# Gated linear attention with a mixture of adapters: loads of v on ScalarE's ring, a gate from negated logits, and a new instruction order

## The chip, the cores and the metric

The kernel runs on one core of one Trainium2 chip. The metric is the device time of one execution in microseconds. TensorE is called PE, VectorE DVE, ScalarE ACT, GpSimd POOL and SyncE SP, as in the profile.

## The reference

Four batches of eight heads, 768 steps, head size 48. First a linear attention with a decay `alpha` for each channel, then a mixture of eight rank-16 adapters, of which each token takes the two with the largest logits.

```python
for t in range(S):
    state = alpha[:, :, t, :, None] * state + np.einsum('bhd,bhe->bhde', k[:, :, t], v[:, :, t])
    y[:, :, t] = np.einsum('bhd,bhde->bhe', q[:, :, t], state)
x = y.transpose(0, 2, 1, 3).reshape(B * S, H * D)        # 3072 x 384
logits = x @ w_gate                                      # 3072 x 8
topk = the 2 largest of each row;  w = softmax over these 2
out = x + sum over the 2 of  w * ((x @ A[e]) @ B[e])
```

## The kernel before, in words

The sequence of a batch is cut into six chunks of 128 steps, so there are 24 units (batch, chunk), numbered `u`. Each unit passes through some thirty stages, each a small function of the same name in the code.

- `ld` loads a whole batch of one input (alpha as `a_t`, then `k_t`, `q_t`, `v_t`), 1.18 MB in runs of 48 floats. There are sixteen loads. `load_engine` says which engine issues each; before, that is SP for all of them. Each input has two buffers (`TURNS`), so a load of batch b waits for the readers of batch b - 2.
- `ln` takes the logarithm of two chunks of alpha (ACT). `cum` sums it along the chunk with a matmul (PE). `eup`, `edn` and `edec` are exponents of the sums (ACT). `kgm` and `qgm` multiply k and q with them, and `vbc` casts v (POOL).
- `tr` transposes kg and qg into one PSUM tile (PE, eight transposes). `kk` copies the k half out (DVE, L481), `qq` the q half (ACT, L486).
- `at` is the score product of a unit, eight matmuls on 48 rows each, two heads side by side in the upper and the lower rows of the array (L510). `msk` applies the causal mask (DVE, L518).
- `sdm` scales the state `kv` of the unit before into `sdec` (DVE, L462), and `kv` adds this unit's k times v (PE, L495 and L500).
- `yt` makes the output transposed: for a chunk after the first four full-size matmuls with `sdec` (L529), then eight matmuls on 64 columns each, two heads side by side in the columns of the array (L534). `xs` copies it to SBUF (ACT).
- `z` is the product with the adapters' A and with the gate (PE). The gate is a chain over the eight logits of a row: `gmx` (the eight values sorted, L571), `gdf` (minus the largest, L576), `gex` (exponent on ACT, L581), `gwu` (keep the two largest, and sum, L587), `grd` (reciprocal), `gzw` (weights times z).
- `zt` transposes that, `zs` copies it (ACT), `qs` and `av` make the untransposed output in the same PSUM bank (L548, L557), `delta` adds the product with B (L618), `fin` copies the sum (ACT, L625), and a store on SP sends it.

Matmuls thus come in three shapes of the array: full, row-tiled (`at`) and column-tiled (the second part of `yt`).

The order of every engine's instructions is written out ahead by a planner. `graph` builds a node for each stage and unit, with the costs in `STAGES` (engine, time on the engine, time to the result, in ns), dependencies from `CHAINS` and buffer reuse from `RINGS`. `list_order` takes the nodes one by one: of those that can begin within 40 ns of the first one it takes the one with the smallest key, unit number minus `LEAD` of the stage. Six PSUM slots are shared by `cum`, `tr`, `kv`, `yt`, `z` and `zt`; `HOLDS` names the readers that free them. Each engine runs its list in order. Semaphore waits are added where data or buffers need them, so the plan fixes the order, and not the times.

At the start four loads are issued from `early`, the adapters' weights come over POOL's queue (`wload`), and `wcast` casts them (DVE). SP's list is the sixteen loads, and then the 24 stores.

Of the kernel before, what the change touches and what calls it, by code (L numbers as in the profile page):

```python
# [30 lines left out]
NU = B * NCH  # L31

# [6 lines left out]
def _bc_mid(src: bass.AP, reps) -> bass.AP:  # L39
# [6 lines left out]
    "ln": ("ACT", 445, 545), "ln2": ("ACT", 765, 865),  # L46
    "cum": ("PE", 300, 466), "edn": ("ACT", 385, 485), "eup": ("ACT", 360, 485),
    "edec": ("ACT", 98, 172), "kgm": ("POOL", 979, 1024), "qgm": ("POOL", 979, 1024),
    "vbc": ("POOL", 461, 506), "tr": ("PE", 450, 620), "kk": ("DVE", 345, 429), "qq": ("ACT", 467, 592),
    "sdm": ("DVE", 497, 581), "kv": ("PE", 340, 500), "at": ("PE", 400, 570),  # L50
    "msk": ("DVE", 1164, 1248), "qs": ("PE", 170, 340), "av": ("PE", 215, 385),
    "yt": ("PE", 460, 630), "xs": ("ACT", 520, 612),
    "z": ("PE", 240, 410), "gmx": ("DVE", 91, 175),
    "gdf": ("DVE", 76, 160), "gex": ("ACT", 107, 232), "gwu": ("DVE", 268, 352),
    "grd": ("DVE", 71, 155), "gzw": ("DVE", 258, 342), "zt": ("PE", 57, 220),
    "zs": ("ACT", 147, 272), "delta": ("PE", 163, 330), "fin": ("ACT", 385, 485),
    "st": ("DMA", 655, 2455),
}
LEAD = {
    "kk": -24.77, "qq": -57.8, "vld": 4.5, "vbc": -57.63, "ln": -134.22, "cum": 14.46,  # L60
    "edn": -17.16, "eup": 17.71, "edec": -44.09, "kgm": 72.83, "qgm": -0.48, "tr": 63.33,
    "kq": -190.71, "sdm": -26.53, "kv": 46.61, "at": 13.93, "msk": -49.61, "qs": -13.02,
    "av": -10.13, "xb": 0.5, "xt": 0.4, "xs": -111.93, "z": 10.45, "zc": -33.57, "gmx": 8.16,
    "gdf": -28.3, "gex": 94.59, "gwu": -38.76, "grd": 76.82, "gw": -7.12, "gzw": -20.75,
    "yt": 41.02, "zt": 22.93, "zs": -73.06, "delta": 44.96, "fin": 36.34, "st": 100,
}
CHAINS = (
    "ln cum eup kgm tr kk at msk yt xs z gmx gdf gex gwu grd gzw zt zs delta fin st",
    "cum edn qgm tr", "cum edec sdm kv", "kgm kv", "vbc kv", "sdm yt", "tr qq at", "qq yt",
# [4 lines left out]
    ("tr", "qgm", QRING), ("kv", "vbc", VRING), ("av", "vbc", VRING), ("at", "kk", 3), ("at", "qq", 8), ("av", "qq", 8),  # L74
    ("msk", "at", 1), ("av", "msk", 5), ("z", "xs", 3), ("delta", "zs", 3), ("st", "fin", 24),
    ("qs", "sdm", SRING), ("kv", "sdm", 1), ("kgm", "cum", 4), ("qgm", "cum", 4), ("at", "tr", 8),
    ("av", "tr", 8), ("z", "yt", 3), ("delta", "zt", 3), ("st", "zt", 24),
# [4 lines left out]
    "yt": (("xs", 0),), "z": (("gzw", 0),), "zt": (("fin", 0),),  # L82
# [7 lines left out]
def list_order(nodes, deps, holds):  # L90
# [19 lines left out]
    order, span = [], 0  # L110
    for _ in nodes:
        best = None
        for e, names in cand.items():
            can = []
            for n in names:
                if n[0] == "ld" and loads[e][nl[e]][1] != n:
                    continue
                s = max(ready[n], free[e])
                if n in holds:
                    if slot[ns % SLOTS] is None:  # L120
                        continue
                    s = max(s, slot[ns % SLOTS])
                can.append((s, n))
# [15 lines left out]
        free[e] = s + nodes[n][1]  # L139
        end = s + nodes[n][2]  # L140
# [34 lines left out]
def load_engine(x):  # L175
    return "ACT" if x in ((0, 1, 0), (0, 3, 0)) else "SP"


def graph(lead):
    nodes, deps = {}, []  # L180

    def has(f, u):
        c = u % NCH
        if not 0 <= u < NU or (f in ("sdm", "edec", "qs") and c == 0):
            return False
# [28 lines left out]
    for x, item in enumerate(load_list()):  # L214
# [3 lines left out]
        t = 1060 if c is not None else 4450  # L218
        nodes[n] = ("DMB" if eng == "POOL" else "DMA", t, t + 1300, x)
# [3 lines left out]
        if eng == "POOL":  # L223
            nodes["is", x] = ("POOL", 1000, 1000, b * NCH + (c or 0) - 6)
            deps.append((("is", x), n))
            n = ("is", x)
        if b >= TURNS[i]:
# [6 lines left out]
    for f, readers in HOLDS.items():  # L234
        for u in range(NU):
            if (f, u) in nodes:
# [24 lines left out]
def kernel(  # L261
# [18 lines left out]
    trsb = ctx.enter_context(tc.tile_pool(name="trsb", bufs=8))  # L280
# [49 lines left out]
    def wcast(_):  # L330
        for hh in range(2):
# [4 lines left out]
            nc.vector.tensor_copy(  # L336
                W[rows, :, E * R:NW], W_st[rows, E * NP * R:].rearrange("f (p e) -> f p e", p=NP))
# [8 lines left out]
    early = [n for n in order if n[0] == "ld"][:4]  # L346
    for n in early:
        ld(n[1])
    nc.scalar.preload_act_table_set("natural_log_exp_and_others")
# [128 lines left out]
    def kk(u):  # L478
        s = st[u]
        s["kk"] = trsb.tile([P, NP, P], F2, name="kk", bufs=3)  # L480
        nc.vector.tensor_copy(out=s["kk"], in_=s["tr"][:, 0])  # L481

    def qq(u):
        s = st[u]
        s["qq"] = trsb.tile([P, NP, P], F2, name="qq")
        nc.scalar.copy(s["qq"], s["tr"][:, 1])  # L486
# [17 lines left out]
    def at(u):  # L504
        s = st[u]
        t = ps_at.tile([P, 2, NP, P], F4, name="at")
        for p in range(NP):
            for hh in range(2):
                rows = slice(HP * hh, HP * hh + D)
                nc.tensor.matmul(  # L510
                    t[:, hh, p, :], s["kk"][rows, p, :], s["qq"][rows, p, :],
# [10 lines left out]

    def yt(u):
        s = st[u]
        b, c = units[u]
        s["yt"] = ps_s.tile([P, NP, P], F4, name="yt", tag="m", bufs=6)
        if c > 0:
            for p in range(NP):
                nc.tensor.matmul(  # L529
                    s["yt"][:, p, :], sdec[u % SRING][:, p].rearrange("p b d -> p (b d)"),  # L530
                    s["qq"][:, p, :], start=(p == 0), stop=False, skip_group_check=True)
# [12 lines left out]
    def qs(u):  # L544
        s = st[u]
        b, c = units[u]
        for p in range(NP):
            nc.tensor.matmul(  # L548
                s["y"][:, p * 2 * D:(p + 1) * 2 * D], s["qq"][:, p, :],
# [23 lines left out]
    def gdf(u):  # L573
        s = st[u]
# [95 lines left out]
```

## Time and profile before

| | |
|---|---|
| median of 3 runs | 107.2 us (106.11 to 107.24) |
| profiled execution | 107.46 us, span 105.8 us |
| PE, matmul | 76.5 us busy, 72% of the span |
| ACT | 74.0 us, 70% |
| DVE | 70.0 us, 66% |
| POOL | 65.3 us, 62% |
| hardware DMA queue | 23.60 MB, 75.0% of 16 engines |
| granted PE clock | 0.998 |

The profile is of one execution. Its span runs from the first to the last instruction, and the device time lies 1.66 us above it. A row of the timeline has the start in us from the span's start, the length, the engine, the line of the code, the operation and its operands. A mark x8 means that eight instructions were merged. A bracket gives idle time of the engine before the row, and the event that ended it. DMA-issuing instructions are on a line of the queue's own (SPq for SP). Matmuls overlap, so the start of the next group tells more than the length of a row.

### The profile page before, as it was taken

To read this page: it belongs to the slowest core of one execution; us is meant where nothing else is said; L and a number is where in the kernel's file an instruction comes from. 1 tells how busy PE (TensorE), PEld (TensorE's weight loads), DVE (VectorE), ACT (ScalarE), POOL (GpSimd) and SP (SyncE) were. 2 spreads that over 40 slices of the span, in tenths; PEclk is the share of its full clock that TensorE was granted. 3 is DMA by queue.
4 is the path that set the end of the run, shared out by engine and by line. 5 is a ranking of instruction groups with operands and counts; after the bars stand their busy time and mean duration, and the time that the engine had idled before them with its cause. 6 is when DMAs were issued, how large, how long until landed. Compare 5 with 4: busy or idle time off the path is not lost.

```text
span 105.8 us, 3378 instructions
## 1 busy us (share of the span) xinstructions
PE 76.5 (72%) x1312; PEld 58.1 (55%) x1312; DVE 70.0 (66%) x229; ACT 74.0 (70%) x201; POOL 65.3 (62%) x103
## 2 busy tenths in 40 slices
PE   0007002397898898989999779889989999798850
PEld 0004001375575775757767568676767777676720
DVE  4002030159989797777998397979678999798810
ACT  4029900095889888896899789696995997665670
POOL 7992029989911959995191999940688794900000
PEclk9999999999999999999999999999999999999999
DMA  0999997979793989789896969698889899421052
GB/s 7 289 209 273 244 286 214 290 212 312 196 287 103 307 223 288 214 246 254 241 286 199 308 172 308 191 287 229 240 263 339 281 336 390 178 80 74 6 209 89
DMA packets 28528, 24.21 MB, mean 229 GB/s; under 512 B 752, under 2 KB 28400, under 8 KB 28512
## 3 DMA queue, kind: packets, MB, share of 16 engines
q1 hardware_dynamic: 28288, 23.60, 75.0%
q0 software_dynamic: 224, 0.41, 2.5%
q8 instruction: 10, 0.16, 0.6%
q14 instruction: 6, 0.05, 0.2%
HBM read 19.28 MB, written 4.72 MB: 227 GB/s over the span
## 4 chain that ended last, share of the span: by engine, by line
DMA 33%; PE 23%; SPq 10%; DVE 10%; ACT 10%; POOL 7%; issue 3%; ACTq 0%; POOLq 0%; DVEq 0%
DMA k_t<-in_k_dram 12%; DMA a_t<-in_alpha_dram 11%; SPq L306 10%; DMA q_t<-in_q_dram 10%; PE tr L475 5%; DVE at_sb L518 4%; POOL qg L450 4%; POOL kg L443 3%; PE yt L534 3%; PE z L565 2%; PE at L510 2%; ACT o L625 2%; ACT qq L486 2%; PE yt L529 2%; ACT zs L614 2%
## 5 line engine op out<-in xcount | busy, mean ns | idle before, releaser
L443 POOL TENSOR_TENSOR kg<-k_t,up 128x384 bf16<-128x384 f32 x24 | 23.7, 1004 | 17.2 <-DMA k_t<-in_k_dram 11.2
L518 DVE TENSOR_TENSOR at_sb<-at,mask 128x1024 bf16<-128x1024 f32 x24 | 29.2, 1217 | 0.7 <-PE at L510 0.6
L450 POOL TENSOR_TENSOR qg<-q_t,dn 128x384 bf16<-128x384 f32 x24 | 23.6, 1006 | 4.7 <-DMA q_t<-in_q_dram 2.4
L486 ACT COPY qq<-tr 128x512 bf16<-128x512 bf16 x24 | 14.2, 594 | 13.2 <-DVE kk L481 11.4
L481 DVE COPY kk<-tr 128x512 bf16<-128x512 bf16 x24 | 9.9, 421 | 12.1 <-PE tr L475 8.3
L542 ACT CAST xs<-yt 128x512 bf16<-128x512 f32 x24 | 14.4, 607 | 3.6 <-PE yt L534 3.6
L409 PE MATMUL cum<-lg,suf 128*128 128x384 bf16 x24 | 8.7, 369 | 8.2 <-ACT lg L400 8.2
L457 POOL CAST vb<-v_t 128x384 bf16<-128x384 f32 x24 | 11.7, 511 | 4.5 <-PE y L557 4.2
L475 PE MATMUL tr<-ident,kg 128*128 128x128 bf16 x96 | 9.9, 230 | 6.2 <-POOL kg L443 6.2
L400 ACT ACTIVATE lg<-a_t 128x768 bf16<-128x768 f32 x12 | 10.1, 860 | 6.1 <-DMA a_t<-in_alpha_dram 6.1
L475 PE MATMUL tr<-ident,qg 128*128 128x128 bf16 x96 | 9.8, 228 | 5.1 <-POOL qg L450 4.8
L625 ACT COPY o<-y 128x384 f32<-128x384 f32 x24 | 11.5, 496 | 1.3 <-PE y L618 1.0
L424 ACT ACTIVATE up<-cum 128x384 f32<-128x384 f32 x24 | 11.6, 504 | 0.3 <-PE cum L415 0.3
L429 ACT ACTIVATE dn<-cum 128x384 f32<-128x384 f32 x24 | 11.5, 508 | 0.0
L510 PE MATMUL at<-qq,kk 48*128 48x128 bf16 x192 | 9.8, 222 | 2.0 <-DVE at_sb L518 1.0
L462 DVE TENSOR_TENSOR sdec<-kv,dec 128x384 bf16<-128x384 f32 x20 | 10.9, 547 | 0.3 <-PE kv L500 0.3
L475 PEld LDWEIGHTS <-kg 128*128 128x128 bf16 x96 | 6.3, 101 | 7.4 <-POOL kg L443 6.3
L565 PE MATMUL z<-W,xs 128*128 128x136 bf16 x96 | 9.5, 223 | 1.0 <-ACT xs L542 0.6
L475 PEld LDWEIGHTS <-qg 128*128 128x128 bf16 x96 | 6.3, 102 | 6.8 <-POOL qg L450 6.8
L534 PE MATMUL yt<-at_sb,vb 128*64 128x128 bf16 x192 | 9.9, 225 | 0.0
L557 PE MATMUL y<-vb,at_sb 128*128 128x48 bf16 x192 | 8.7, 183 | 0.4 <-ACT zs L614 0.4
L618 PE MATMUL y<-B_all,zs 128*128 128x384 bf16 x24 | 7.7, 327 | 1.1 <-ACT zs L614 1.0
(58 smaller groups left out, 152.7 us busy)
## 6 DMA issues: line engine op xcount, KB each, us to landing
out_dram<-o SPq DMA_DIRECT2D x24, 192.0 KB, 2.3
W_st<-in_moe_A_dram POOLq DMA_DIRECT2D x2, 96.0 KB, 6.1
B_st<-in_moe_B_dram POOLq DMA_DIRECT2D x1, 192.0 KB, 6.9
a_t<-in_alpha_dram SPq DMA_DIRECT2D x4, 0.2 KB, 10.3
k_t<-in_k_dram SPq DMA_DIRECT2D x4, 0.2 KB, 10.9
q_t<-in_q_dram SPq DMA_DIRECT2D x4, 0.2 KB, 10.9
v_t<-in_v_dram SPq DMA_DIRECT2D x4, 0.2 KB, 10.5
W_st<-in_moe_w_gate_dram POOLq DMA_DIRECT2D x2, 6.0 KB, 5.5
```

The costliest lines, as they stand in the source:

```text
L424: nc.scalar.activation(s["up"].rearrange("p h d -> p (h d)"), s["cum"][:, 0:DM], AF.Exp)
L443: nc.gpsimd.tensor_tensor(out=s["kg"][:, :, 0:D], in0=batches[b][1][:, c], in1=s["up"], op=ALU.mult)
L450: nc.gpsimd.tensor_tensor(out=s["qg"][:, :, 0:D], in0=batches[b][2][:, c], in1=s["dn"], op=ALU.mult)
L457: nc.gpsimd.tensor_copy(out=s["vb"][:, :, 0:D], in_=batches[b][3][:, c])
L475: nc.tensor.transpose(t[:, w, p, :], pair(src, p), ident[:, :])
L486: nc.scalar.copy(s["qq"], s["tr"][:, 1])
L510: nc.tensor.matmul(t[:, hh, p, :], s["kk"][rows, p, :], s["qq"][rows, p, :], start=True, stop=True)
L518: nc.vector.tensor_tensor(out=s["at_sb"].rearrange("p a b t -> p (a b) t"), in0=s["at"].rearrange("p a b t -> p (a b) t"), in1=_bc_mid(mas ...
L534: nc.tensor.matmul(s["yt"][HP * hh:HP * hh + HP, p, :], s["vb"][:, 2 * p + hh, :], s["at_sb"][:, hh, p, :], start=(c == 0 and p == 0), sto ...
L542: nc.scalar.copy(s["xs"], s["yt"])
L565: nc.tensor.matmul(s["z"], s["xs"][:, p, :], W[:, p, :], start=(p == 0), stop=(p == NP - 1))
L625: nc.scalar.copy(s["o"], s["y"])
```

## The change

The four loads of v are issued by ACT, on its own DMA ring, at places in ACT's list that the planner picks; SP keeps the twelve others. Three loads, those of alpha, k and q of the first batch, are issued ahead of everything else.

The gate's weights are negated when they are cast. The sorted logits then have the two wanted ones at their end. The exponent reads z itself, with scale -1 and the largest logit's negated value as a bias, so `gdf` is gone, and `gwu` compares the other way.

The transposes are copied into one tile `kq` of eight blocks: DVE copies five (k's four and q's first), ACT the other three. It has six buffers, where kk had three and qq eight.

The products with `sdec` leave `yt` and become a stage `ys`, which can be placed apart from the column-tiled products. The planner's PE charges 97 ns for a change between full, row-tiled and column-tiled, and 600 ns more where `at` is followed by anything but `yt`. Costs and `LEAD` values are new, and so is the order on all engines.

```diff
 STAGES = {
-    "tr": ("PE", 450, 620), "kk": ("DVE", 345, 429), "qq": ("ACT", 467, 592),
-    "at": ("PE", 400, 570), "yt": ("PE", 460, 630), "gdf": ("DVE", 76, 160),
+    "tr": ("PE", 448, 620), "kk": ("DVE", 338 + 67 * SPL, 421 + 67 * SPL),
+    "qq": ("ACT", 475 - 107 * SPL, 594 - 107 * SPL),
+    "at": ("PE", 240, 405), "ys": ("PE", 224, 400), "yt": ("PE", 245, 420),
...
+TILES = {"at": 1, "yt": 2}
+RETILE = 97
+AFTROW = 600
...
 CHAINS = (
-    "ln cum eup kgm tr kk at msk yt xs z gmx gdf gex gwu grd gzw zt zs delta fin st",
-    "cum edn qgm tr", "cum edec sdm kv", "kgm kv", "vbc kv", "sdm yt", "tr qq at", "qq yt",
+    "ln cum eup kgm tr kk at msk yt xs z gmx gex gwu grd gzw zt zs delta fin st",
+    "cum edn qgm tr", "cum edec sdm kv", "kgm kv", "vbc kv", "sdm ys yt", "tr qq at", "qq ys", "kk ys",
...
                 s = max(ready[n], free[e])
+                if e == "PE" and TILES.get(n[0], 0) != tiled:
+                    s = max(s, free[e] + RETILE + (AFTROW if tiled == 1 and n[0] != "yt" else 0))
...
 def load_engine(x):
-    return "ACT" if x in ((0, 1, 0), (0, 3, 0)) else "SP"
+    return "ACT" if x[1] == 3 else "SP"
...
-        t = 1060 if c is not None else 4450
-        nodes[n] = ("DMB" if eng == "POOL" else "DMA", t, t + 1300, x)
+        t = (1060 if c is not None else 3950) + (2600 if x == 0 else 0)
+        if x in (1, 2):
+            t += 500
+        nodes[n] = ("DMB" if eng == "POOL" else "DMA", t, t + 1500, x)
...
-        if eng == "POOL":
-            nodes["is", x] = ("POOL", 1000, 1000, b * NCH + (c or 0) - 6)
+        if eng != "SP":
+            nodes["is", x] = (eng, 900, 900, b * NCH + (c or 0) - 6)
             deps.append((("is", x), n))
             n = ("is", x)
+            dep(("ld", x - 2), n)
...
-            nc.vector.tensor_copy(
-                W[rows, :, E * R:NW], W_st[rows, E * NP * R:].rearrange("f (p e) -> f p e", p=NP))
+            nc.vector.tensor_scalar(
+                W[rows, :, E * R:NW], W_st[rows, E * NP * R:].rearrange("f (p e) -> f p e", p=NP),
+                -1.0, None, ALU.mult)
...
-    early = [n for n in order if n[0] == "ld"][:4]
+    nc.scalar.preload_act_table_set("natural_log_exp_and_others")
+    early = [("ld", x) for x in range(3)]
     for n in early:
         ld(n[1])
-    nc.scalar.preload_act_table_set("natural_log_exp_and_others")
...
     def kk(u):
-        s["kk"] = trsb.tile([P, NP, P], F2, name="kk", bufs=3)
-        nc.vector.tensor_copy(out=s["kk"], in_=s["tr"][:, 0])
+        nc.vector.tensor_copy(
+            out=s["kq"][:, 0:NP + SPL], in_=s["tr"].rearrange("p w a t -> p (w a) t")[:, 0:NP + SPL])
...
     def qq(u):
-        s["qq"] = trsb.tile([P, NP, P], F2, name="qq")
-        nc.scalar.copy(s["qq"], s["tr"][:, 1])
+        nc.scalar.copy(
+            s["kq"][:, NP + SPL:], s["tr"].rearrange("p w a t -> p (w a) t")[:, NP + SPL:])
...
+    def ys(u):
+        s = st[u]
+        s["yt"] = ps_s.tile([P, NP, P], F4, name="yt", tag="m", bufs=6)
+        for p in range(NP):
+            nc.tensor.matmul(
+                s["yt"][:, p, :], sdec[u % SRING][:, p].rearrange("p b d -> p (b d)"),
+                s["kq"][:, NP + p, :], start=(p == 0), stop=False, skip_group_check=True)
...
-    def gdf(u):
-        s["df"] = moep.tile([P, E], F4, name="df")
-        nc.vector.tensor_scalar(s["df"], s["z"][:, E * R:NW], s["mx"][:, 0:1], None, ALU.subtract)
...
-        nc.scalar.activation(s["ex"], s["df"], AF.Exp)
+        nc.scalar.activation(
+            s["ex"], s["z"][:, E * R:NW], AF.Exp, bias=s["mx"][:, E - 1:E], scale=-1.0)
...
-            out=s["wu"], in0=s["z"][:, E * R:NW], scalar=s["mx"][:, 1:2], in1=s["ex"],
-            op0=ALU.is_ge, op1=ALU.mult, accum_out=s["den"])
+            out=s["wu"], in0=s["z"][:, E * R:NW], scalar=s["mx"][:, E - 2:E - 1], in1=s["ex"],
+            op0=ALU.is_le, op1=ALU.mult, accum_out=s["den"])
```

## The prediction

> **What bounds the kernel now.** I read the page's shares first, then the chain of work that ended last, then SyncE's own timeline, POOL's timeline, and last the PE timeline, group by group.
>
> ```profile
> span 105.8 us, 3378 instructions
> PE 76.5 (72%) x1312; PEld 58.1 (55%) x1312; DVE 70.0 (66%) x229; ACT 74.0 (70%) x201; POOL 65.3 (62%) x103
> DMA 33%; PE 23%; SPq 10%; DVE 10%; ACT 10%; POOL 7%; issue 3%; ACTq 0%; POOLq 0%; DVEq 0%
> ```
>
> No engine is full, and the chain is DMA for a third, so the stages have to be taken apart. The chain in order of time shows where its DMA part ends:
>
> ```profile
> 66.41 10.44 DMA q_t<-in_q_dram
> ...
> 77.01 1.97 POOL qg L450 x2
> ...
> 80.94 0.40 PE tr L475 x4
> ```
>
> The third column names the work. The last load on the chain is q of the fourth batch, which lands at 76.9 us. What follows, 26 us, is mostly PE. SyncE's timeline says what set that landing:
>
> ```profile
> 0.87 0.84 SPq L306 DMA_DIRECT2D a_t<-in_alpha_dram  x1
> 2.17 3.81 SPq L306 DMA_DIRECT2D k_t<-in_k_dram  x1
> 6.43 5.41 SPq L306 DMA_DIRECT2D q_t<-in_q_dram  x1
> ...
> 66.41 4.23 SPq L306 DMA_DIRECT2D q_t<-in_q_dram  x1
> 71.10 4.42 SPq L306 DMA_DIRECT2D v_t<-in_v_dram  x1
> ```
>
> The sixteen loads (start, duration) follow each other with a pitch of (71.10 - 22.31) / 10 = 4.9 us from the sixth to the sixteenth. The first took 0.84 us to issue, into an empty ring; the later ones took 3.8 to 5.5 because the ring was full. So SP waits for the DMA engines and not they for SP, at 19.5 us a batch of four loads. PE needs 76.5 / 4 = 19.1 us a batch. The two are matched, and POOL shows how closely:
>
> ```profile
> 38.52 1.97 POOL L450 TENSOR_TENSOR qg<-q_t,dn 128x384 bf16<-128x384 f32 x2 [1.19 <-DMA q_t<-in_q_dram]
> 77.00 1.97 POOL L450 TENSOR_TENSOR qg<-q_t,dn 128x384 bf16<-128x384 f32 x2 [1.19 <-DMA q_t<-in_q_dram]
> ```
>
> In the second and the fourth batch q is taken up as it lands (the bracket is idle time and its releaser). The windows (length, PE, PEld, DVE, ACT, POOL busy, PE clock, DMA share, GB/s) give the rates:
>
> ```profile
> 2.50:5.00 2.50, 0.00 (x0) 0.00 (x0) 0.00 (x0) 0.00 (x0) 2.36 (x15) 1.00 0.98 277
> 20.00:75.00 55.00, 48.97 (x844) 37.55 (x844) 44.92 (x133) 45.42 (x124) 38.97 (x51) 1.00 0.87 246
> 77.00:103.00 26.00, 22.94 (x409) 17.30 (x405) 21.38 (x77) 19.43 (x57) 12.98 (x17) 1.00 0.62 216
> ```
>
> After q has landed PE is busy 22.9 of 26 us: it sets the end. In the long middle it is busy 49.0 of 55, and the DMA engines 0.87. PE's own timeline shows what a switch of tile shape costs:
>
> ```profile
> 91.25 0.33 PE L500 MATMUL kv<-vb,kg 128*128 128x96 bf16 x4
> 91.42 0.39 PE L529 MATMUL yt<-qq,sdec 128*128 128x128 bf16 x4
> 91.73 0.41 PE L534 MATMUL yt<-at_sb,vb 128*64 128x128 bf16 x8
> 92.08 0.40 PE L510 MATMUL at<-qq,kk 48*128 48x128 bf16 x8
> ```
>
> Read start to start: the four kv take 0.17, but the four sdec products ahead of the 64-column ones take 0.31, where four transposes of the same size, between full-size groups, take 0.23 in this timeline. Groups of kv, qs, delta and z are likewise 0.09 to 0.10 longer when a row- or column-tiled group follows: kv 0.17 and 0.26, delta 0.16 and 0.26, z 0.24 and 0.33. A switch costs about 0.095 us.
>
> **What the Trainium skill says.** "TensorEngine Tiling (Array Packing)", Key Properties, says that changing the tiling mode drains TensorE; the 0.095 us above agree in kind, and the trace gives the price. "DMA: Bandwidth & Descriptors", Issuing engines are not separate DMA queues, says that DMAs of the scalar, sync and gpsimd engines end on the same 16 DMA engines and interleave, so that a second issuer saves only issue time. The same page, Queues, rings and completion order, says that SP and ACT own a ring each on every DMA engine, and that an engine goes round-robin between rings packet by packet. The trace before has one hardware ring in use and cannot confirm this for SP beside ACT. On a second ring bringing no rate the trace is not so clear: from 10 to 12.5 us, with POOL's weight loads on their own queue, the windows show a share of 1.17 and 295 GB/s, against 0.87 and 246 later.
>
> **The change part by part.**
>
> *Tile switches.* I went through PE's order in both kernels and counted changes between full groups, row-tiled `at` and column-tiled `yt`: 94 before, 69 after, because `at` goes straight into another unit's `yt` 17 times and the sdec products, now `ys`, are kept away from `yt`. 25 x 0.095 = 2.4 us of PE time less, about 1 a unit. PE instructions stay at 1312. PE is the limit both in the middle, where it keeps pace with the loads, and in the tail, so I count it whole. If the loads remain the limit in the middle, only the tail's seven units count: 7 x 0.095 = 0.7.
>
> *Gate.* `df` goes: 24 x 220 ns = 5.1 us of DVE, and in the last unit's chain 0.22 plus a handover of 0.05 = 0.27 us of the end. The exponent now reads z in PSUM with a bias. `dec`, an exponent of the same 128x8 from PSUM, takes 214 ns and `ex` 217, so I take no difference (bounds: minus 0.02 to plus 0.1 us for the bias operand). The negation in `wcast` is an operation of the 174 ns kind, long before the first z: nothing.
>
> *kq.* DVE copies 640 columns of the transposes where it copied 512, ACT 384 where it copied 512. ACT's slope from `xs` (512 columns, 607) and `zs` (128, 282) is 0.85 ns a column: 24 x 0.108 = 2.6 us less. For DVE, at_sb (1024, 1217) and sdec (384, 547) give a fixed part of 145 ns, so the copy's 421 is 0.54 ns a column: 24 x 0.069 = 1.7 us more. DVE's balance is 5.1 - 1.7 = 3.4 us less. Neither DVE nor ACT is the bound, so no gain is booked. `at` waits for both copies as before. Eight buffers of qq and three of kk become six of kq: units are six apart there, a batch, and I book nothing.
>
> *v on ACT.* Four issues move from SP to ACT. Each is a shape move (about 0.35 on SP) and a DMA_DIRECT2D; into an empty ring SP paid 0.84. So 4 x 1.2 = 4.8 us more on ACT, against 2.6 saved: plus 2.2. No DMA issue of ACT is in the trace, so the bounds are 0.8 (nearest row) and 4.3 us (a full ring) each. I take 0.84, since v's previous load is a batch away and its ring is empty by then. Behind each issue wait the `xs`, `up` or `zs` copies that follow it on ACT; 1.2 us is inside ACT's slack in the middle (45.4 busy of 55).
>
> *Order of landing.* This counts more. By ACT's new order v is issued after 4 `up` and 4 `dn`, then after 8, 13 and 18 `up`; the old trace had ACT there at about 12, 33, 51 and 68 us. SP issued v at 12.3, 33.0, 51.9 and 71.1, but behind 5 us or more of earlier bytes. On its own ring v starts at once and takes packets from the q that is in service. With rings served in turn and no more rate, v3 from 68 to 78 us would push q3, and q3 would land with the last bytes at about 81 instead of 76.9. With more rate it is offset: with a full ring ahead of it the first load ran at 277 GB/s, against 246 in the middle, a share of 0.98 against 0.87. Two rings have twice the packets waiting. If four v flights of 9 us run at 277, the stream gains 36 x (1 - 246/277) = 4.0 us by its end, which takes back q3's 4. I take both: q3 at about 77, the stream complete at 77.5. The bounds for q3 are 73 (SP's q goes first) and 81 (no extra rate).
>
> *Sum.* Minus 2.4 for switches, minus 0.27 for the gate's last chain, zero for ACT, zero for the loads: minus 2.7 on the profiled execution's 107.46 us gives 104.8. That execution lies 0.26 above the median of 107.2, so 104.5.
>
> **Rivals.** *The loads hide PE's gain.* q lands as now, PE catches up sooner and waits longer for it. Then only the tail's 0.7 and the gate's 0.27 remain: 106.2. For it speaks the matched pace of 19.5 and 19.1 us; against it that PE still has 22.9 us of work at q's landing, over a unit more than the fourth batch needs.
>
> *Both gain.* The stream comes 4 us sooner and q3 lands at 73; PE then sets everything. It starts with the first `tr` of qg at 20.2 and needs 72 us from there, with 6 us of waits; a third of the waits goes with the loads. 2.7 + 2 = 4.7 us less: 102.5. For it the 277 and 295 GB/s; against it the skill's page.
>
> *q behind v (slower).* No extra rate, and round-robin holds q back in each batch: q3 lands near 81, 4.2 us late. The tail shrinks by its own 1.0 and by PE's backlog of about 1.5. Plus 4.2 minus 2.5 = 1.7 us: 108.9. It decides from a landing later than 79.5, where the delay exceeds what PE gains. POOL's wait for q at 38.5 and 77.0 speaks for it, since there is no slack to absorb a late q.
>
> *ACT blocked (slower).* The issue takes 4.3 us when the DMA engines are loaded, as on SP. Three of the four fall in ACT's busy middle and hold its copies back by some 3 us net each: plus 9 minus 2.7, 113.5. Against it stands the 0.84 of the first issue.
>
> **How the numbers follow.** Forecast 104.5 (own range 103.3 to 105.7): 0.32. Both gain, 102.5: 0.20. Loads hide it, 106.2: 0.19. q behind v, 108.9: 0.21. ACT blocked, 113.5: 0.08. A change of 1% or 1.1 us is about what a measurement of this kernel can tell from none: 106.1 and 108.3 are the borders. Faster takes the forecast and both gain, with a little of the third: 0.54. Same takes most of the third and the edge of q behind v: 0.22. Slower: 0.24. The range leaves out ACT blocked and the far ends: 101.8 to 109.6.
>
> **What would show it.** ACT's row of DMA_DIRECT2D near 0.84 us (right) or near 4 (blocked). The windows from 20 to 75 with more than 260 GB/s, and q's last landing at 77 or before. PE busy near 74 us, with `at` followed by `yt`. PE's share in the tail at 0.9 or more. I am wrong in the main step if POOL's waits for q_t or k_t grow beyond 6 us in total, or if q3 lands after 79.5.

## The result, and the profile after

The changed kernel took 111.03 us (median of 4, 110.88 to 111.53) against 107.22 for the kernel before (median of 4 beside it): a ratio of 1.040, with a 95% interval from 1.031 to 1.049. It is slower. Single executions of one kernel differed by several per cent in the runs that followed; the ratios leave out the disturbed ones, while medians are over all. Measured three times more, the same program had medians of 109.79, 108.50 and 109.69 us, beside 107.86, 107.99 and 107.76 for the kernel before. Its median was higher each time, but by 0.5 to 1.9 us and not by 3.8, so this first loss is the largest of four.

The profiled execution took 111.11 us. First its page, the lines that answer to those shown before, and the granted PE clock in 40 slices:

```profile
span 109.4 us, 3350 instructions
PE 75.7 (69%) x1312; PEld 60.0 (55%) x1312; DVE 70.2 (64%) x205; ACT 72.2 (66%) x205; POOL 65.9 (60%) x103
PEclk9999999999999999999975558999999999999995
DMA 27%; PE 18%; ACT 17%; DVE 16%; SPq 13%; issue 3%; POOL 3%; ACTq 0%; POOLq 0%; DVEq 0%
L597 ACT ACTIVATE ex<-z,mx 128x8 f32<-128x8 f32 x24 | 6.4, 287 | 3.9 <-DVE mx L592 2.7
```

PE is busy for 0.8 us less and the span is 3.6 us longer, so PE stands 4.4 us more. The clock row has something new: four slices in the middle at half speed. The timelines of the two DMA queues, of POOL and of PE say what happened ahead of them. SP's loads (start, duration), and ACT's:

```profile
6.86 4.70 SPq L318 DMA_DIRECT2D q_t<-in_q_dram  x1
...
34.56 8.17 SPq L318 DMA_DIRECT2D k_t<-in_k_dram  x1
43.19 5.39 SPq L318 DMA_DIRECT2D q_t<-in_q_dram  x1
49.04 8.53 SPq L318 DMA_DIRECT2D a_t<-in_alpha_dram  x1
```

```profile
10.98 0.84 ACTq L318 DMA_DIRECT2D v_t<-in_v_dram  x1
32.57 0.70 ACTq L318 DMA_DIRECT2D v_t<-in_v_dram  x1
47.10 0.70 ACTq L318 DMA_DIRECT2D v_t<-in_v_dram  x1
73.12 0.70 ACTq L318 DMA_DIRECT2D v_t<-in_v_dram  x1
```

ACT's issue costs 0.70 to 0.84 us. SP's issue, where the second and the third v are in flight on the other ring, is stretched to 8.2 and 8.5. The third v is issued 3.9 us after the third q and has landed at 54.3 us; that q lands at 58.9. The DMA packets of the window from 50 to 52 us show why:

```profile
DMA packets 828, 0.64 MB, mean 318 GB/s; under 512 B 0, under 2 KB 828, under 8 KB 828
q10 hardware_dynamic: 828, 0.64, 106.1%
```

Here q10 is ACT's ring (on the page it has moved 4.72 MB, the four v) and q1 SP's. For two microseconds every packet is v's, while q stands in the other ring.

The chain of waits gives q's whole way from issue to landing (third column: what the time was spent on), then POOL's and PE's timelines where it lands:

```profile
6.86 13.34 DMA q_t<-in_q_dram
...
43.19 15.70 DMA q_t<-in_q_dram
```

```profile
20.34 2.91 POOL L463 TENSOR_TENSOR qg<-q_t,dn 128x384 bf16<-128x384 f32 x3 [2.55 <-DMA q_t<-in_q_dram]
...
59.02 1.95 POOL L463 TENSOR_TENSOR qg<-q_t,dn 128x384 bf16<-128x384 f32 x2 [6.50 <-DMA q_t<-in_q_dram]
```

```profile
54.10 0.40 PE L488 MATMUL tr<-ident,kg 128*128 128x128 bf16 x4
60.07 0.61 PE L488 MATMUL tr<-ident,qg 128*128 128x128 bf16 x4 [5.57 <-POOL qg L463]
```

These are the transposes of the third batch's first unit. In the kernel before:

```profile
47.20 4.18 SPq L306 DMA_DIRECT2D q_t<-in_q_dram  x1
...
57.74 0.40 PE L475 MATMUL tr<-ident,kg 128*128 128x128 bf16 x4
58.83 0.40 PE L475 MATMUL tr<-ident,qg 128*128 128x128 bf16 x4 [0.69 <-POOL qg L450]
```

Now PE reaches them 3.64 us sooner, and q is ready 1.24 us later, although it was issued 4.0 us sooner. The sum of the first two, 4.88, is the whole growth of the stand from 0.69 to 5.57. PE runs its list in order, and 15 or so groups of other units, whose inputs were there, stand behind these transposes.

The windows give the price (length, PE, PEld, DVE, ACT, POOL, clock, DMA share, GB/s), the last line being the kernel before:

```profile
20.00:75.00 55.00, 44.75 (x759) 35.96 (x759) 39.63 (x104) 40.19 (x115) 38.54 (x48) 0.91 0.91 256
55.00:60.00 5.00, 0.00 (x0) 0.00 (x0) 0.66 (x6) 0.26 (x1) 0.98 (x2) 0.59 0.65 180
60.00:65.00 5.00, 4.93 (x55) 4.05 (x56) 2.75 (x6) 2.77 (x10) 3.37 (x5) 0.50 0.94 268
75.00:103.00 28.00, 25.90 (x491) 20.61 (x486) 25.03 (x80) 22.50 (x67) 15.40 (x20) 1.00 0.48 164
60.00:65.00 5.00, 4.13 (x82) 3.61 (x80) 4.03 (x20) 4.51 (x15) 5.00 (x6) 1.00 0.85 239
```

From 60 to 65 us PE is busy all the time and gets 55 instructions done, against 82 in the same window before. It runs at half clock until 66.2 us: 6.1 us of work at half speed, so by my estimate 3.1 us lost. "TensorE: Matmul & The Clock Gate", section What's actually happening, of the Trainium skill says that the clock falls to half after one or more idle windows of about 3.4 us. The length agrees: the half clock lasts from about 55.95 to 66.2 us, 10.2 us, which is three times 3.41. "Idle" doesn't: in the 3.41 us ahead of the drop PE was busy for 1.78 us.

### The profile page after: what moved, and what is told of

It is laid out like the page before. It is cut to its first block, busy times and chain, and to the rows that moved or that the text cites. A ratio compares the mean times of both kernels' runs of the same rounds, so it can differ in the third digit from the quotient of the medians.

```text
span 109.4 us, 3350 instructions
## 1 busy us (share of the span) xinstructions
PE 75.7 (69%) x1312; PEld 60.0 (55%) x1312; DVE 70.2 (64%) x205; ACT 72.2 (66%) x205; POOL 65.9 (60%) x103
## 3 DMA queue, kind: packets, MB, share of 16 engines
q10 hardware_dynamic: 6208, 4.72, 15.5%
HBM read 19.28 MB, written 4.72 MB: 219 GB/s over the span
## 4 chain that ended last, share of the span: by engine, by line
DMA 27%; PE 18%; ACT 17%; DVE 16%; SPq 13%; issue 3%; POOL 3%; ACTq 0%; POOLq 0%; DVEq 0%
DMA q_t<-in_q_dram 27%; SPq L318 13%; DVE at_sb L535 8%; PE tr L488 4%; ACT xs L563 3%; ACT o L642 3%; DVE kq L495 3%; PE at L527 3%; ACT kq L502 2%; DVE sdec L475 2%; ACT up L437 2%; ACT lg L413 2%; PE y L635 2%; POOL qg L463 2%; PE y L578 2%
## 5 line engine op out<-in xcount | busy, mean ns | idle before, releaser
L502 ACT COPY kq<-tr 128x384 bf16<-128x384 bf16 x24 | 11.8, 503 | 12.8 <-DVE kq L495 12.2
L495 DVE COPY kq<-tr 128x640 bf16<-128x640 bf16 x24 | 11.5, 485 | 12.4 <-PE tr L488 11.0
L488 PE MATMUL tr<-ident,qg 128*128 128x128 bf16 x96 | 10.2, 235 | 11.7 <-POOL qg L463 11.7
L563 ACT CAST xs<-yt 128x512 bf16<-128x512 f32 x24 | 13.9, 607 | 0.7 <-PE yt L555 0.7
L413 ACT ACTIVATE lg<-a_t 128x768 bf16<-128x768 f32 x12 | 10.2, 864 | 6.0 <-DMA a_t<-in_alpha_dram 6.0
L488 PEld LDWEIGHTS <-qg 128*128 128x128 bf16 x96 | 6.9, 105 | 12.5 <-POOL qg L463 12.5
L442 ACT ACTIVATE dn<-cum 128x384 f32<-128x384 f32 x24 | 12.0, 524 | 0.0
L527 PE MATMUL at<-kq 48*128 48x128 bf16 x192 | 10.0, 225 | 2.1 <-DVE at_sb L535 2.1
L555 PE MATMUL yt<-at_sb,vb 128*64 128x128 bf16 x192 | 9.0, 224 | 0.2 <-POOL vb L470 0.2
L597 ACT ACTIVATE ex<-z,mx 128x8 f32<-128x8 f32 x24 | 6.4, 287 | 3.9 <-DVE mx L592 2.7
```

The lines of the kernel that those rows point to most:

```text
L488: nc.tensor.transpose(t[:, w, p, :], pair(src, p), ident[:, :])
L495: nc.vector.tensor_copy(out=s["kq"][:, 0:NP + SPL], in_=s["tr"].rearrange("p w a t -> p (w a) t")[:, 0:NP + SPL])
L502: nc.scalar.copy(s["kq"][:, NP + SPL:], s["tr"].rearrange("p w a t -> p (w a) t")[:, NP + SPL:])
L527: nc.tensor.matmul(t[:, hh, p, :], s["kq"][rows, p, :], s["kq"][rows, NP + p, :], start=True, stop=True)
L563: nc.scalar.copy(s["xs"], s["yt"])
```

## Experiments

My theory after these traces: v on its own ring overtakes the q that still waits in SP's ring, and the new PE order, planned for loads of 3.95 us each, stands at that q. Rivals: the ring alone, the order alone, the gate, the lower clock.

**The ring and the order, one without the other.** The changed order with v back on SP, behind q; and, measured twice, the old order with v on ACT.

```diff
 # e1_v_on_sp, from the changed kernel (v is put behind q in SP's list)
-    return "ACT" if x[1] == 3 else "SP"
+    return "SP"
 # e2_before_v_act and e13_before_v_act_again, from the kernel before
-    return "ACT" if x in ((0, 1, 0), (0, 3, 0)) else "SP"
+    return "ACT" if x[1] == 3 else "SP"
+    spot = {3: ("dn", 4), 7: ("up", 8), 11: ("dn", 13), 15: ("up", 18)}
```

> Every engine's order as in the changed kernel, but the four loads of v go back to SP, each behind the q of its batch. Theory queue jump (v on its own ring is served ahead of the k and q that already wait on SP's ring, and the new order puts tr of unit 12 ahead of other ready work, so PE stands still for q of the third batch and its clock halves): q of batches 3 and 4 land near 57.6 and 77 us again, the stand at tr 12 shrinks from 5.6 to some 3 to 4 us because the order still asks for q early, and the time is 108 to 110. Theory order alone (the new order is worse whoever loads v): 110 to 112. Theory ring alone (the order is fine, the second ring does all the harm): 103 to 105.5.

> The kernel before with one edit: the four loads of v are issued by ACT, behind the 4th dn, the 8th up, the 13th dn and the 18th up, as in the changed kernel. Queue jump: the q loads of batches 1 to 3 land 1 to 3 us later than before, the old order has other work ahead of tr 12 and loses only part of it: 107.5 to 109.5. Order alone: 107 (no change). Ring alone: 110.5 to 111.5, all of the loss.

> e2_before_v_act once more (the old order, v on ACT), since only one undisturbed run of it was seen. Second ring alone costs little with the old order: 107.5 to 108.5, with the last load in at 76 us and not at 82. Second ring does the harm: 110 to 112.

The changed order on one ring: median 110.83 beside 107.66, ratio 1.023 (1.011 to 1.035). The stand at the q transposes, which I had expected at 3 to 4 us, is gone, and another took its place, at a `cum` whose alpha now comes later, with the clock at half from 50.2 to 57.1 us. From its PE timeline:

```profile
49.10 0.32 PE L456 MATMUL cum<-lg,suf 128*128 128x384 bf16 x1 [1.39 <-ACT lg L447]
```

The old order with v on ACT: 1.038 (1.023 to 1.053) the first time, a ratio that rests on one execution, and 1.012 (1.007 to 1.016) the second time, with medians of 108.16 and 107.86. The second rests on many more executions. Its windows:

```profile
20.00:75.00 55.00, 48.79 (x847) 37.95 (x848) 45.37 (x133) 45.79 (x128) 39.81 (x51) 1.00 0.95 272
```

The loads run at 272 GB/s instead of 246 and PE does no more than before (48.79 of 55 us; it was 48.97). In this order a faster stream gains nothing, and PE had no wait over 0.9 us after 21 us. So neither half alone gains: the order costs some 2%, the ring about 1% by the second measurement. The loss isn't one of bandwidth.

**The clock.** A hundred more k transposes while PE waits for q, to keep the clock up; and, on the variant with v on SP, seven products of zeros ahead of the `cum` that waits. Neither leaves anything out.

```diff
 # e4_warm, in tr
-        for w, src in enumerate((s["kg"], s["qg"])):
+        for w, src in enumerate((s["kg"], s["qg"])) if u != 12 else enumerate((s["kg"],) * 26 + (s["qg"],)):
+            w = int(src is s["qg"])
 # e6_sp_warm_cum12, e1 and in cum
-        for _ in range(0):
+        for _ in range(7 if u == 12 else 0):
```

> The changed kernel, in which PE repeats the four kg transposes of unit 12 another 25 times (100 matmuls of 128 columns, about 5.6 us) while it would stand and wait for qg of unit 12. If the halved clock from 57 to 67 us costs what the windows suggest (some 6 us of PE work at half rate), the clock stays at 1.0 and the time falls by 2.5 to 3.5 us to about 108. If the clock is only a companion of the stand and the lost time is made up later, it stays at 110.5 to 111.5.

> As e1_v_on_sp (v back on SP, all else as changed), and PE runs seven 512-column products of zeros (some 1.5 us) into the bank of cum 12 ahead of it, where it stood 1.4 us for the logarithm before its clock fell to half from 50.4 to 57 us. Theory clock (most of what was lost with v on SP is the 6.6 us at half clock, 3.3 us of PE work): the clock stays near 1.0 and the time falls to 105.5 to 107. If the half clock costs nothing because others bound then: 109 to 110 as in e1.

The first kept the clock at 1.00 from 55 to 67 us, and the later pair of q products on POOL began at 69.46 instead of 72.11, 2.65 us sooner, close to the 3.1 worked out above. Its time is no measure of that (median 114.58): the fourth v then stood on ACT for a store, and PE, which was waiting for what ACT had still to do, stood for 3.6 us until 76.5. ACT's timeline:

```profile
74.38 0.02 ACT L318 MOVE_SHAPE v_t<-in_v_dram  x1 [3.33 <-DMA out_dram<-o]
```

The second gave 1.015 (1.004 to 1.026), not clearly better than without the products; waits of 2.77 and 2.88 us for q came up instead. The size of the clock's share thus rests on the windows and on the first part of one trace. The 32 executions of the changed program (the first four, e10, e16, and e18, which turned out to be the same program) point the same way. In 19 of them the mean granted clock is under 0.98, and their median is 110.48 us; in the other 13 it is 108.18, close to the 107.22 to 107.99 of the kernel before. This is no proof of the price, since the stand that lowers the clock costs time by itself.

**The plan's price for a load.**

```diff
 # e7_act_4450
-        t = (1060 if c is not None else 3950) + (2600 if x == 0 else 0)
+        t = (1060 if c is not None else 4450) + (2600 if x == 0 else 0)
```

> The changed kernel with one number back: the planner takes 4450 ns for a load and not 3950, so the orders of all engines are planned for a slower stream (tr of unit 12 comes behind delta 8 by itself; 72 tile switches and not 69). Queue jump with an order that asks for q too early: no stand of over 2 us in the middle, 104.5 to 107. If the second ring does the harm whatever the order: 109.5 to 111.5. A possible trap: the semaphore of v of the fourth batch is now shared with the first store, so ACT could stand at it for 2 to 3 us.

Median 112.07, ratio 1.021 (1.012 to 1.030), where I had expected 104.5 to 107. No stand of PE beyond 1.5 us after 21 us and the clock at 1.00 in all middle windows, and still no gain. From the last unit's k transposes to the end it needs 17.5 us (91.41 to 108.9), the changed kernel 15.1. A new price makes a new order on every engine, so this run can't say what the price alone does.

**The transposes that stand, moved.** The first unit of the third batch, its transposes and their two copies, go behind 16 ready stages.

```diff
 # e5_tr_later, e11_tr_later_again, e17_tr_later_3
+def tr_later(order, u=12, behind=("delta", 8)):
+    move = [n for n in order if n in (("tr", u), ("kk", u), ("qq", u))]
+    out = [n for n in order if n not in move]
+    k = out.index(behind) + 1
+    return out[:k] + move + out[k:]
-    order = plan()[1]
+    order = tr_later(plan()[1])
 # e12_tr_half: behind=("kv", 10).   e8_tr_later_v0_sp: and the first v on SP, behind q
```

> The changed kernel, with tr of unit 12 (and its two copies) moved on PE behind the 16 stages that follow it there, up to delta of unit 8. Queue jump with the early tr: PE has about 3.5 us of that work to do while q lands at 59, stands 2 us in place of 5.6, keeps its clock, and the time is 106.5 to 108. If the loss lies in late loads and not in what PE does meanwhile: 110.5 to 111.5.

> As e5_tr_later, but v of the first batch is issued by SP behind q of that batch; the other three stay on ACT. Queue jump at the start: the first qg begins at 19.1 as in the kernel before and not at 20.3 or later, and the time is 1.0 to 1.5 us below e5's undisturbed runs, 103.5 to 105. If the late start is made up later: as e5, 105 to 106.

> The changed kernel itself, on the chip that also runs the next three. Again 110.5 to 111.5, with a stand of 5 to 6 us at tr of unit 12 and a half clock for some 9 us after it. If the stand belonged to one chip's loads only, it is shorter here and the time nearer to 109.

> e5_tr_later once more (tr of unit 12 and its two copies behind delta of unit 8), beside the changed kernel. Theory early tr: 104.8 to 106.5, some 5 us below the changed kernel, with no stand of over 2 us between 50 and 62 us. If the earlier result came from a lucky run: 108 to 110.

> As before, but tr of unit 12 moves only behind kv of unit 10, seven stages with some 1.6 us of PE work, and not sixteen. Theory early tr: the stand shrinks from 5.6 to about 4 us, still long enough for the clock to fall; 108.5 to 110. If only the length of the work ahead counts and the clock not: 109.4 (minus 1.6). If a stand of this length no longer halves the clock: 106 to 107.

Side by side on one chip: the changed kernel 109.79 (1.011, 0.998 to 1.023), with the stage moved 106.16 (0.979, 0.967 to 0.991). PE's timeline of the first and then POOL's and PE's of the second:

```profile
59.98 0.61 PE L488 MATMUL tr<-ident,qg 128*128 128x128 bf16 x4 [4.77 <-POOL qg L463]
```

```profile
57.75 1.95 POOL L470 TENSOR_TENSOR qg<-q_t,dn 128x384 bf16<-128x384 f32 x2 [6.30 <-DMA q_t<-in_q_dram]
...
58.80 0.40 PE L495 MATMUL tr<-ident,qg 128*128 128x128 bf16 x4 [1.46 <-POOL qg L470]
```

POOL waits for q as long as ever. PE no longer does, since it has the other stages to run. The clock is at half for 3.4 us here, against 6.8 in the first. Of the 3.8 us between the two spans 1.5 were there before these transposes (unit 11's began at 51.02 and 49.48), where a v landed later in the first. The half move gave 1.009 (1.004 to 1.014), no difference from the changed kernel that these runs can tell; its trace has no stand at this q, so it doesn't test the length of the move. With the first v on SP the first q product began at 18.51 us, sooner than the 19.11 of the kernel before, but the ratio was 0.998 (0.990 to 1.007).

**The gate alone, on the kernel before** (`df` dropped, weights negated, exponent with a bias):

```diff
 # e9_gate_only
-        nc.scalar.activation(s["ex"], s["df"], AF.Exp)
+        nc.scalar.activation(
+            s["ex"], s["z"][:, E * R:NW], AF.Exp, bias=s["mx"][:, E - 1:E], scale=-1.0)
```

> The kernel before with the gate edit alone (negated gate weights, df gone, the exponent reads z with a bias); order otherwise untouched. Prediction's step: minus 0.27 us, 106.9. Theory that the bias operand makes the exponent dearer (287 ns in the changed kernel's trace against 217): ACT gains 24 x 70 ns = 1.7 us of work, and the end is 0 to 0.5 us later, 107.2 to 107.7. Theory that DVE mattered (5 us less): 105.5 to 106.5.

Median 107.16 beside 108.20, ratio 0.987 (0.978 to 0.997), from three of five executions; the means over all are 108.67 and 108.52. A gain of a per cent is possible and not shown. `ex` takes 284 ns in it instead of 217.

**The place of v.** The first and the third v were to be issued later on ACT, with PE's order untouched.

```diff
 # e14_v2_later (e15: with tr_later; e18: only the first v, behind ("edn", 3); e19: both)
+def v2_later(order, behind=("edn", 12)):
+    out = [n for n in order if n != ("ld", 11)]
+    k = out.index(behind) + 1
+    return out[:k] + [("ld", 11)] + out[k:]
 # e16_changed_3: the changed kernel
```

> The changed kernel with one edit: the issue of v of the third batch moves down ACT's list, to behind the dn of the third batch's first unit (51.3 us in the changed kernel's own trace, where it was issued at 47.1). PE's order is the changed kernel's. Theory A (v overtakes q on the other ring): q of the third batch has the rings to itself until 51 and lands at 53 to 55 instead of 59.0; the stand of PE at the first q transpose of that batch falls from 4.8 to 5.6 us to under 1.5, and the time by 3 us or more, to 106 to 107.5, near the kernel with that transpose moved. Rival B (the new PE order alone; v's place is not what makes q late): q stays at 57.5 to 59, the stand at 4 us or more, the time within 1 us of the changed kernel. Rival C (v is then late): q lands at 54, but PE stands 2 us or more for vb, and less than half is won back.

> The changed kernel with both edits: v of the third batch issued behind the dn of that batch's first unit, and the transposes of that unit and their two copies behind the 16 stages that were ready. If A is the whole cause, the two edits mend the same stand and both together give no more than the better one alone (within 0.7%). If the order itself costs something beyond the stand, both together are 1% or more better than the later v alone. If v then comes late, the sum is worse than the moved transposes alone.

> The changed kernel again, on the same chip as the others of this call: 109 to 111 us, the stand of 4.8 to 5.6 us at the first q transpose of the third batch wherever v is issued at 46 to 48 us.

> The changed kernel with the transposes of the third batch's first unit moved behind 16 ready stages, again: 105 to 106.5 us, 0.98 of the kernel before, as in the two earlier calls.

> The changed kernel with one edit: v of the first batch is issued behind the fourth dn instead of ahead of the dn group, so at 12.5 to 13 us instead of 10.4 to 11.3, after SP is through with the issue of q of the first batch. In the traces so far POOL's wait for that q was 1.0 to 2.6 us where v's issue began 0.1 to 0.6 us before the end of q's issue, and 3.3 to 4.3 us where it began 1.0 to 2.2 us before. Theory A (v overtakes the q that is still in its ring): q of the first batch is never overtaken, the first q transpose starts at 19 to 20.5 us in the profile; v of the third batch is then issued at 46 to 48 us, q of that batch is overtaken, PE stands 4 us or more at its first transpose, and the time is 109 to 111. Rival B (the landing of the first q has nothing to do with v's issue): the first q transpose starts as late as 23.5 to 24.5 us in an execution such as those of the last call, and the time is as the changed kernel's, 108 to 109.

> Both v issues later, PE's order untouched: v of the first batch behind the fourth dn, v of the third batch behind the dn of that batch's first unit. Theory A: q of the first batch is early (first q transpose at 19 to 20.5 us) and q of the third lands at 53 to 56 us, the stand of PE there is under 2 us, the granted clock stays at 0.98 or more, and the time is 104.5 to 106.5, 3 us or more below the kernel with only the first v moved. Rival (the new PE order alone makes the stand, wherever v is): the stand stays at 4 us or more and the two kernels of this call are within 1%. Rival C (v of the third batch is then late itself): q is early, but PE stands 2 us or more for the cast v, and less than half is gained.

I had placed these edits wrongly. The first v already stood behind the fourth `dn`, so e18 is the changed kernel once more, instruction for instruction; in e14, e15 and e19 the third v moved one copy of `kq` (about 0.5 us) ahead, and so not later at all. The edits don't test the overtaking. They do show that one program has two courses. From e18, ACT's timeline and queue, then POOL's and PE's:

```profile
10.64 0.84 ACTq L326 DMA_DIRECT2D v_t<-in_v_dram  x1
...
11.02 1.65 ACT L450 ACTIVATE dn<-cum 128x384 f32<-128x384 f32 x4
```

```profile
6.71 5.38 SPq L326 DMA_DIRECT2D q_t<-in_q_dram  x1
12.54 8.94 SPq L326 DMA_DIRECT2D a_t<-in_alpha_dram  x1
```

```profile
22.97 2.91 POOL L471 TENSOR_TENSOR qg<-q_t,dn 128x384 bf16<-128x384 f32 x3 [3.37 <-DMA q_t<-in_q_dram]
...
24.02 0.61 PE L496 MATMUL tr<-ident,qg 128*128 128x128 bf16 x4 [6.61 <-POOL qg L471]
```

Here v was issued 1.4 us before SP had done with q's issue, the first q landed late (16.1 us after its issue), PE's first q transposes began 3.9 us later than before (20.16), and nothing stood long in the third batch. The profiled executions with this order and v on ACT, in us (the first six with PE's order of the changed kernel, then five with the stage moved, e12 by half; e4, with its added work, is left out):

| execution | first v issued | end of q's issue on SP | POOL waits for first q | first q transposes | third v issued | longest stand of PE in 40 to 65 | time |
|---|---|---|---|---|---|---|---|
| changed | 10.98 | 11.56 | 2.55 | 21.39 | 47.10 | 5.57 for q | 111.11 |
| e10 | 11.01 | 11.34 | 1.18 | 20.17 | 47.81 | 4.77 for q | 110.48 |
| e16 | 10.41 | 12.36 | 3.34 | 24.46 | 52.08 | 1.22 for v | 108.30 |
| e18 | 10.64 | 12.09 | 3.37 | 24.02 | 52.66 | 1.21 for v | 108.92 |
| e14 | 10.78 | 11.76 | 3.31 | 23.66 | 52.78 | 1.26 for v | 109.48 |
| e19 | 10.82 | 11.95 | 3.31 | 23.79 | 55.37 | 3.85 for v | 112.00 |
| e11 | 11.27 | 11.38 | 1.14 | 19.88 | 46.27 | 1.46 for q | 106.75 |
| e5 | 10.52 | 12.39 | 3.43 | 24.39 | 54.76 | 2.63 for v | 111.99 |
| e17 | 10.33 | 12.52 | 3.62 | 24.43 | 54.93 | 2.73 for v | 112.27 |
| e15 | 10.42 | 12.05 | 3.29 | 23.96 | 50.77 | 1.06 for v | 108.41 |
| e12 | 10.80 | 11.90 | 4.26 | 23.71 | 53.39 | 1.87 for v | 110.55 |

Where v is issued under 0.6 us before the end of q's issue, the first q is early, the third is overtaken, and the moved stage helps (the early course). Where it is issued about 1 us or more before, the first q itself is overtaken and PE starts 3 to 4 us late; then the third q is there before PE wants it (the late course). In the five traces with the first v on SP behind q (before, e1, e6, e8, e9) the first q lands between 18.1 and 19.1 us, in the fifteen with v on ACT between 18.7 and 23.3.

That v is what delays q can be read from the landings of all twenty traces, batches 2 to 4. Where no v was in flight on ACT's ring while SP issued q, q took 9.8 to 12.3 us from issue to landing (39 loads); where one was, 13.1 to 17.9 (21 loads). The two ranges don't touch. In e15 the late course put the third v 0.6 us behind the end of q's issue, and there q went first. Its packets from 46 to 55 us, and q's way from issue to landing:

```profile
q1 hardware_dynamic: 2875, 2.20, 88.8%
q_t<-in_q_dram SPq DMA_DIRECT2D x1, 0.2 KB, 10.4
```

No packet of ACT's ring is among them, and q took 10.4 us. So the delay by v is shown; which q suffers from it differs among executions.

The times: e18 gave 1.022 (1.003 to 1.041), e16 had a median of 108.50 beside 107.99 for the kernel before, e14 109.43, e19 1.017 (1.000 to 1.033). The moved stage had 0.986 (0.979 to 0.993), 0.979 (0.967 to 0.991) and 1.016 (1.001 to 1.031) in three measurements; the medians are 108.00, 106.16 and 109.12 beside 107.66, 107.86 and 107.99. These ratios rest on three, two and one executions. With the third v moved too (e15) it had 0.986 (0.978 to 0.993), from four of twenty executions, and a median of 107.05 beside 107.99. Whether the moved stage gains anything in the late course is thus open, and no version surely beats the kernel before.

## Why the prediction was wrong

*The failing step is the order of landing.* It put the whole effect of v's ring into the last q, "q3 at about 77". That q landed at 72.6 us, just below the lower bound of 73, since two rings did carry more (256 GB/s in the changed kernel and 272 in the old order, against 246). But v takes what it gets from the q in service, and it did so in the third batch (15.7 us from issue to landing, against 10.4 before) and, in the late course, in the first (16.1 in e18, against 12.2). So the sum's "zero for the loads" is the term that failed: in its place PE stood for 5.57 us at the third q, where it had stood for 0.69, and the clock came on top. The two statements on rings that the prediction cites were no help as it used them. A second ring saved more than issue time. And the rings were not simply served in turn: from 50 to 52 us ACT's had all 828 packets, while in e10 from 52 to 55 us the two had 608 and 606. The step never asked at which q PE would stand. In the new order PE's place for each batch's first q transposes, set beside that q's landing, would have shown it: PE came there 3.64 us sooner and q 1.24 us later.

*Tile switches counted whole.* The order was taken as 25 switches less and otherwise neutral. That the new order is built around other arrival times was not priced, and in one course PE stands for 5.57 us in it. The 2.4 us can't be read from PE's busy time, which is 76.1 us in e18 and 74.6 in e16, one program at full clock, against 76.5 before. From the first q transposes to PE's last matmul it is 79.9 us in e18 and 78.8 in e16, against 82.3 before, so a gain of that size may be there and be eaten by the late start; but a late start also finds more inputs landed, and no run separates the two. From the last batch's first k transposes to the end it is 27.6 us in the changed kernel, e11 and e18 alike (81.82 to 109.4, 77.39 to 105.0, 79.61 to 107.2), and 28.2 before (77.63 to 105.8). The orders differ, so this is rough: 0.6 us of gain, where the tail's own terms, 0.7 and 0.27, made 0.97. That is near to what the rival "loads hide it" left of the gain.

*The clock had no term.* It was at 0.998 before, and I asked of no stand what it would do to the clock. By the estimate above it took 3.1 us.

*The rivals.* "q behind v" had the right mechanism and the wrong place: it was to decide from a last landing after 79.5 us, which came at 72.6. Its 108.9 is near to what the course with the late first q gives (108.3 and 108.92), but by luck: it was made of a late last q, and that q came early. "ACT blocked" fell: 0.70 to 0.84 us an issue.

*What held.* The issue on ACT at 0.84; a faster stream, though at 256 GB/s and not the 260 that I named (272 in the old order); `kq` at 485 ns on DVE and 503 on ACT, where 490 and 486 follow from the steps. The sign of being wrong, POOL's waits for q_t or k_t beyond 6 us in total, was set badly, since the kernel before was beyond it:

```profile
L443 POOL TENSOR_TENSOR kg<-k_t,up 128x384 bf16<-128x384 f32 x24 | 23.7, 1004 | 17.2 <-DMA k_t<-in_k_dram 11.2
L450 POOL TENSOR_TENSOR qg<-q_t,dn 128x384 bf16<-128x384 f32 x24 | 23.6, 1006 | 4.7 <-DMA q_t<-in_q_dram 2.4
```

```profile
L456 POOL TENSOR_TENSOR kg<-k_t,up 128x384 bf16<-128x384 f32 x24 | 24.1, 1012 | 13.9 <-DMA k_t<-in_k_dram 6.5
L463 POOL TENSOR_TENSOR qg<-q_t,dn 128x384 bf16<-128x384 f32 x24 | 23.7, 1002 | 9.5 <-DMA q_t<-in_q_dram 9.1
```

The first two lines are before, the others after. What grew is the wait for q; that for k shrank. Two readings in the prediction were off as well: 24 x 220 ns is 5.3 us and not 5.1, and from the first q transposes PE needed 82.3 us before, 73.9 busy and 8.4 standing, and not 72.

*The gate.* No difference was taken for `ex`, with plus 0.1 us as a bound. It is 287 ns against 217, 70 more in each unit. "ScalarE: Activation LUTs", What ACT_TABLE_LOAD costs, has the price that I missed: with a pointer as bias about 280 ns + 0.83 ns a column, 287 for 8 columns. In spite of it the ratio of the gate alone is a gain of 1.3% (0.3 to 2.2), more than my 0.27 us, if it holds; no trace here says where.

*Open.* What decides the course of an execution: the first v's issue differs by about 1 us among executions. Why the ACT ring's bytes go ahead of what SP's ring holds in one place and share with it in another. Whether v issued after the end of q's issue in every batch makes the kernel faster: q then lands in time, as the landings show, but no run has it throughout, since the edits meant for it moved nothing or the wrong way.

## What to carry to other kernels

When a transfer moves to a ring of its own, price it at every consumer that still waits in the old ring, not at the stream's end, and write the landing of each beside the place where an in-order engine first needs it. A new static order and the arrivals that it was planned for are one thing: test each without the other. A stand of TensorE can cost more than its length (5.57 us here, and by estimate 3.1 more at half clock), so where it can't be avoided, put ready work ahead of the wait.

## What the runs showed of the hardware

- The half clock came in multiples of 3.41 us: 10.2 in the changed kernel, 6.8 in e10 and e1, 3.4 in e11. PE need not be idle for the whole window before it: in the 3.41 us ahead of the drop it was busy 1.78 us in the changed kernel, 0.70 in e10, 1.09 in e11, and 2.02 in e1, where the stand itself was 1.39 us. A stand of 1.48 us in e7 left the clock alone.
- A DMA issue on ACT went ahead of activations that stand before it. In the program it stands behind four `dn`; in e18 it began at 10.64 us and the first of these at 11.02.
- With v in flight on ACT's ring, issues on SP that mostly take 4 to 5 us took up to 9 (8.17 and 8.53 in the changed kernel, 8.94 in e18).
- A load on SP's ring was overtaken by one issued later on ACT's: in the changed kernel q was issued at 43.2 us and landed at 58.9, v at 47.1 and 54.3. q took 13.1 to 17.9 us from issue to landing where a v was in flight while SP issued it, and 9.8 to 12.3 where none was (batches 2 to 4, 60 loads).
- With v on a second ring, in the old order, the DMA engines moved 272 GB/s from 20 to 75 us (e13; 270 in e2), against 246 on one ring.
